# Small-tile matmuls of an attention step in two bursts instead of three

## The chip, the cores and the metric

The kernel runs on one core of a Trainium2 chip. The metric is the device time of one execution in microseconds. Most executions of one kernel agree within about 0.3%; a few here are up to 1% longer, at a granted TensorE clock of 0.989 to 0.996. A profile is one such execution with the hardware profiler on; its span is about 2 us shorter than the time of the run.

## The reference

```python
def _attn_ref(q, k, v):                       # (8, 12, 448, 64) each
    scores = scale * np.matmul(q, k.transpose(0, 1, 3, 2))
    attn = np.maximum(scores, 0.0) ** 2 / S   # squared relu, no softmax
    return np.matmul(attn, v)
...
def _moe_ref(x, w_tok1, w_tok2, w_ch1, w_ch2):  # x: (8, 448, 768), from the heads
    h = np.maximum(x.transpose(0, 2, 1) @ w_tok1, 0.0) @ w_tok2   # over tokens
    u = x + h.transpose(0, 2, 1)
    return u + np.maximum(u @ w_ch1, 0.0) @ w_ch2                 # over channels
```

## The kernel before

The work goes in 24 steps of four heads. In each step run at once: seven score tiles of this step, the values product of the step before (its inputs are squared relus), the transposes of q and k for the next step, and the two token products of the step before. Two channel layers fill TensorE in between: "first-layer" units of 6 matmuls with 448 columns (ScalarE takes the result out of PSUM) and "second-layer" units of 12 with 384 (VectorE takes it). Scores, values and q/k transposes use 64x64 tiles of the array, four at a time, and so does the last part of the first token product in steps 7 and later; all else uses the array whole. TensorE's results land in a memory called PSUM. A channel unit takes one of two banks of it, called "bank" in the code and token banks below; the unit after the next needs the same bank, and can start only when the result has been taken out (evicted).

```python
# PSUM: score tiles 2 x 2 banks, acc0 and acc1 one bank each, two token banks ("bank")
ps_att = ...tile_pool(name="ps_att", bufs=2, space=PSUM)
ps_acc = ...tile_pool(name="ps_acc", bufs=1, space=PSUM)
ps_mm  = ...tile_pool(name="ps_mm", bufs=2, space=PSUM)

def scores(i, c, alone=False):          # 4 matmuls 64*64 into one of two buffers
    ...
    if alone: nc.vector.tensor_scalar(out=at, in0=ps[:, :, :S], scalar1=0.0, ..., op0=ALU.max)
    else:     nc.scalar.activation(at, ps[:, :, :S], AF.Relu)
    squares.append(at)

def square(keep=0):                     # VectorE, in place
    while len(squares) > keep: ...

def fill(share, least=0, upto=0):       # as many channel units as the share asks for
    ...

for i in range(DB + 1, ND + 2):         # steps 4 to 25; "slow" is i <= 6
    scores(i, 0); scores(i, 1)
    values(i - 1, range(QC)); values_out(i - 1)
    scores(i, 2)
    ...                                 # first filler
    square()
    if i - 1 >= XDMA: fill(0.37, least=1)
    scores(i, 3); scores(i, 4)
    transposes(i + 1)                   # into acc0, acc1; both copies on VectorE
    square()
    if slow: token1(i - 1); fill(1 / 3, least=1)
    else:    fill(0.37, least=1, ...); token1_main(i - 1)
    if not slow: token1_rest(i - 1)
    scores(i, 5); scores(i, 6)
    if not slow: square(); fill(0.1, least=1)
    token2(i - 1)                       # its addition is VectorE's
    square()
    fill(1 / 3 if slow else 0.16, least=1)
```

(The step is cut: the conditions at both ends, the loads and the transposes of x are left out.)

Of the kernel before, what the change touches and what calls it, by code (L numbers as in the profile page):

```python
# [16 lines left out]
def kernel(  # L17
# [19 lines left out]
    ND = B * H // 4  # L37
    DB = H // 4
    QC = S // 64
# [83 lines left out]
    qkT, at2, squares, accs = {}, {}, [], {}  # L123
# [60 lines left out]
    def scores(i, c, alone=False):  # L184
        sb = qkT[i]
        ps = ps_att.tile([128, 2, 512], FP32, tag="att", name="sc_ps")
        for r in range(2):
            for g in range(2):
                h = slice(64 * g, 64 * (g + 1))
                nc.tensor.matmul(  # L190
                    ps[64 * r : 64 * (r + 1), g, :S],
                    lhsT=sb[h, r, 1, c * 64 : (c + 1) * 64],
                    rhs=sb[h, r, 0, :],
                    start=True,
                    stop=True,
                    skip_group_check=True,
                )
        at = attn.tile([128, 2, S], BF16, name="at", bufs=12)
        if alone:
            nc.vector.tensor_scalar(  # L200
                out=at, in0=ps[:, :, :S], scalar1=0.0, scalar2=None, op0=ALU.max
            )
        else:
            nc.scalar.activation(at, ps[:, :, :S], AF.Relu)  # L204
        squares.append(at)
        at2[i, c] = at

    def square(keep=0):
        while len(squares) > keep:
            at = squares.pop(0)  # L210
            nc.vector.tensor_tensor(out=at, in0=at, in1=at, op=ALU.mult)  # L211

    def values(i, cs):
        v_raw = raws[i, "v"]
        if i not in accs:
            accs[i] = [ps_acc.tile([128, 512], FP32, tag=f"acc{r}", name="acc_ps") for r in range(2)]
        ps = accs[i]
        for c in cs:
            at = at2.pop((i, c))
            for r in range(2):  # L220
                for g in range(2):
                    h = slice(64 * r, 64 * (r + 1))
                    nc.tensor.matmul(  # L223
                        ps[r][64 * g : 64 * (g + 1), :S],
                        lhsT=v_raw[h, g, c, :],
                        rhs=at[h, g, :],
                        start=(c == 0),
                        stop=(c == QC - 1),
                        skip_group_check=True,
                    )  # L230

    def values_out(i, split=False):
        b, d = divmod(i, DB)
        ps = accs.pop(i)
        for r in range(2):
            if split and r == 1:
                nc.scalar.activation(
                    xT[b % 2][:, 2 * d + r, :S], ps[r][:, :S], AF.Copy, scale=float(alpha2)
                )
                continue  # L240
            nc.vector.tensor_scalar(  # L241
                out=xT[b % 2][:, 2 * d + r, :S],
                in0=ps[r][:, :S],
                scalar1=float(alpha2),
                scalar2=None,
                op0=ALU.mult,
            )
        if i > 2 * DB - 1:
            for r in range(2):
                nc.vector.tensor_scalar(  # L250
                    out=xT[b % 2][:, 2 * d + r, S:],
                    in0=ps[r][:, S - 64 : S],
                    scalar1=float(alpha2),
                    scalar2=None,
                    op0=ALU.mult,
                )
# [3 lines left out]
    XDMA = 8  # L260
# [28 lines left out]
    def token1(i):  # L289
        x_sb = x_tiles.pop(i)  # L290
        ps = ps_mm.tile([128, JC, 256], FP32, tag="bank", name="t1_ps")
        for j in range(JC):
            for c in range(4):
                nc.tensor.matmul(  # L294
                    ps[:, j, :],
                    lhsT=wt1[:, c, j * 128 : (j + 1) * 128],
                    rhs=x_sb[:, :, c, :],
                    start=(c == 0),
                    stop=(c == 3),
                )  # L300
        r1 = mix.tile([128, JC, 256], BF16, name="r1_sb")
        nc.scalar.activation(r1, ps, AF.Relu)
        r1_tiles[i] = r1

    def token1_main(i):
        x_sb = x_tiles[i]
        t1s[i] = ps = [
            ps_acc.tile([128, 512], FP32, tag=f"acc{j}", name="t1_ps2") for j in range(JC)
        ]
        for j in range(JC):  # L310
            for c in range(3):
                nc.tensor.matmul(  # L312
                    ps[j][:, :256],
                    lhsT=wt1[:, c, j * 128 : (j + 1) * 128],
                    rhs=x_sb[:, :, c, :],
                    start=(c == 0),
                    stop=False,
                    skip_group_check=True,
                )

    def token1_rest(i):

        x_sb, ps = x_tiles.pop(i), t1s.pop(i)
        for m in range(2):
            cols = slice(64 * m, 64 * (m + 1))
            for j in range(JC):
                h = slice(64 * j, 64 * (j + 1))
                nc.tensor.matmul(  # L328
                    ps[j][cols, :256],
                    lhsT=wt1_last[h, cols] if j else wt1[h, 3, cols],  # L330
                    rhs=x_sb[h, :, 3, :],
                    start=False,
                    stop=True,
                    skip_group_check=True,
                )
        r1 = mix.tile([128, JC, 256], BF16, name="r1_sb")
        for j in range(JC):
            nc.scalar.activation(r1[:, j, :], ps[j][:, :256], AF.Relu)  # L338
        r1_tiles[i] = r1
# [179 lines left out]
    def fill(share, least=0, upto=0):  # L519
        if not queue:  # L520
            return
        credit[0] += share * rate[0]
        done = 0
        while queue and (credit[0] > 0 or done < least or since[0] < upto):
            cost, unit = queue.pop(0)
            credit[0] -= cost
            since[0] += cost
            unit()
            done += 1


# [70 lines left out]
    i = DB  # L602
# [31 lines left out]
    for i in range(DB + 1, ND + 2):  # L634
        slow = i <= 2 * DB
        back = i - 1 < ND
        if i == 2 * DB + 1:
            rate[0] = (EC * C1 + NT * C2) / DB
        if i < ND:
            scores(i, 0)  # L640
            scores(i, 1)
        if 0 <= i - 1 < ND:
            values(i - 1, range(QC))
            values_out(i - 1)
        if i < ND:
            scores(i, 2)
        if i - 1 < XDMA:
            fill(1 / 3, least=1)
        if 0 <= i - 1 < ND:
            x_back(i - 1)  # L650
        since[0] = 0.0
        if i > 2 * DB + 1:
            if i == 2 * DB + 2:
                hold_back(1, x_tiles[i - 1][:1, 0, 0, :1])
            while u_later and u_later[0] < max(i - 1 - (i == 2 * DB + 2), 0):
                u_back(u_later.pop(0))
        if i + PRE < ND:
            if i - 1 >= XDMA:
                nc.gpsimd.tensor_copy(gate, x_tiles[i - 1][:1, 1, 3, 127:])  # L659
            load_four(i + PRE)  # L660
        if i == 5:
            load_wc2(1, 2)
            load_wt1_last()
        square()
        if i - 1 >= XDMA:
            fill(0.37, least=1)
        if i < ND:
            scores(i, 3)
            scores(i, 4)
        if i + 1 < ND:  # L670
            transposes(i + 1)
        square()
        if slow:
            token1(i - 1)
            fill(1 / 3, least=1)
        else:
            fill(0.37, least=1, upto=4400 if back else 0)
            if back:
                token1_main(i - 1)
        if i < ND:  # L680
            if not slow:
                token1_rest(i - 1)
            scores(i, 5)
            scores(i, 6)
        elif back:
            token1_rest(i - 1)
        if not slow:
            square()
            fill(0.1, least=1)
        if back:  # L690
            token2(i - 1)
            if (i - 1) % DB == DB - 1:
                channel_work((i - 1) // DB)
        if i == 2 * DB + 1:
            hold_back(0, uT_tiles[1][:1, 0, :1])
            for _ in range(DB):
                u_back(u_later.pop(0))
        square()
        fill(1 / 3 if slow else 0.16, least=1)
# [32 lines left out]
```

## Time and profile before

| | before |
|---|---|
| median time | 376.2 us |
| TensorE busy | 365.0 of 374.7 us |
| VectorE, ScalarE busy | 212.1, 211.0 us |
| steps 4 to 6 (41.5 to 69.75 us) | 28.25 us, TensorE busy 28.07 |

Below, "burst" is a run of small-tile matmuls without a whole-array one in it. Its length is the difference of two starts in the timeline: its first score tile's and that of the whole-array matmul behind it. In the kernel before, the first burst of a step takes 2.02 us (202.86 to 204.88 in the lines that the prediction shows) and the second 0.98 (206.94 to 207.92). A length counts the way out of the small tiles, but not the way in, 0.10. One joined burst has one way in less, so it is compared with 2.02 + 0.98 + 0.10 = 3.10 us.

Seven steps have a wait in the first burst. This is the timeline of one (start, length, engine, line, idle before):

```profile
229.89 0.63 DVE L211 TENSOR_TENSOR at<-at 128x896 bf16<-128x896 bf16 x1 [0.19 <-ACT at L204]
230.43 1.15 DVE L363 TENSOR_TENSOR uT_sb<-h_ps,xT 128x448 bf16<-128x448 f32 x2
...
231.32 1.83 PE L223 MATMUL acc_ps<-at,v_raw 64*64 64x448 bf16 x28
```

VectorE squares the score tiles 5 and 6 first, and stands idle before each until ScalarE's relu is done (the square shown is the second). The token addition (L363) follows and ends at 231.58. The values product wants acc0 and acc1, which the addition empties, and takes 1.83 us where it takes 1.49 without that wait. The burst becomes 2.35 us instead of 2.02.

### The profile page before, as it was taken

Reading aid. Unit: us, or ns where it says so; the run is one execution under the profiler, and the core shown is the slowest. Engines: PE = TensorE matmul, PEld = TensorE weight load, DVE = VectorE, ACT = ScalarE, POOL = GpSimd, SP = SyncE. Lnnn points to the kernel's source line nnn. Section 1 sums busy time; section 2 is a strip of 40 time slices with the busy share of each in tenths; the row PEclk is TensorE's granted clock in tenths of the full one; section 3 lists DMA queues with packets and bytes.
Section 4 is the critical chain, followed back from the end, with each engine's and each line's share of the span. In section 5 each row is a group of like instructions: output and inputs, shape, how many; then the busy total and the mean of one; then the engine's idle time right before and its main releaser. Section 6 shows DMA issues by size and latency. Waiting matters only on the chain.

```text
span 374.7 us, 10236 instructions
## 1 busy us (share of the span) xinstructions
PE 365.0 (97%) x4377; PEld 201.2 (54%) x4377; DVE 212.1 (57%) x414; ACT 211.0 (56%) x313; POOL 99.1 (26%) x185
## 2 busy tenths in 40 slices
PE   7889999999999999999999999999999999999996
PEld 3544555455555655565455655555555654555554
DVE  2986688756576666475554684575555755131022
ACT  3987888776345468725775457752775456311400
POOL 8956348304212403430330304412210000000000
PEclk9999999999999999999999999999999999999999
DMA  8999999923998886756765877758560534233024
GB/s 150 118 197 163 179 206 172 180 39 67 128 174 171 159 146 95 115 104 154 97 101 90 117 141 132 108 80 158 107 99 13 93 87 98 58 69 87 0 54 116
DMA packets 69566, 43.32 MB, mean 116 GB/s; under 512 B 43473, under 2 KB 66065, under 8 KB 69521
## 3 DMA queue, kind: packets, MB, share of 16 engines
q0 software_dynamic: 24496, 21.49, 40.8%
q1 hardware_dynamic: 44640, 20.75, 26.6%
q8 instruction: 34, 0.56, 0.6%
q10 hardware_dynamic: 384, 0.43, 0.4%
q14 instruction: 12, 0.09, 0.1%
HBM read 43.42 MB, written 11.01 MB: 145 GB/s over the span
## 4 chain that ended last, share of the span: by engine, by line
PE 89%; DVE 6%; ACT 1%; DMA 1%; issue 1%; POOL 0%; ACTq 0%; POOLq 0%; DVEq 0%
PE m_ps L443 29%; PE m_ps L404 28%; PE acc_ps L223 9%; PE sc_ps L190 9%; PE h_ps L353 4%; PE t_ps L312 3%; DVE at L211 2%; PE qkT_ps L140 2%; PE t_ps L294 1%; DMA q_raw<-in_q_dram 1%; DVE uT_sb L363 1%; PE t_ps L328 1%; ACT at L204 1%; DVE qkT L154 1%; PE x_ps L276 1%
## 5 line engine op out<-in xcount | busy, mean ns | idle before, releaser
L204 ACT ACTIVATE at<-sc_ps 128x896 bf16<-128x896 f32 x167 | 144.8, 924 | 49.7 <-PE sc_ps L190 49.7
L211 DVE TENSOR_TENSOR at<-at 128x896 bf16<-128x896 bf16 x168 | 97.7, 619 | 55.9 <-ACT at L204 55.9
L404 PE MATMUL m_ps<-uT_sb,wc 128*128 128x448 bf16 x564 | 115.5, 353 | 0.2 <-DVE uT_sb L363 0.2
L443 PE MATMUL m_ps<-wc,r_sb 128*128 128x384 bf16 x660 | 113.2, 326 | 0.0
L443 PEld LDWEIGHTS <-r_sb 128*128 128x128 bf16 x660 | 62.7, 98 | 46.7 <-issue 6.1
L411 ACT ACTIVATE r_sb<-m_ps 128x448 bf16<-128x448 f32 x94 | 51.3, 546 | 56.0 <-PE m_ps L404 55.6
L404 PEld LDWEIGHTS <-wc 128*128 128x128 bf16 x564 | 52.3, 98 | 53.4 <-issue 8.3
L450 DVE TENSOR_TENSOR out_sb<-m_ps,u_sb 128x384 f32<-128x384 f32 x55 | 30.5, 554 | 48.1 <-PE m_ps L443 48.1
L190 PE MATMUL sc_ps<-qkT 64*64 64x448 bf16 x672 | 53.2, 358 | 1.1 <-ACT at L204 0.9
L223 PE MATMUL acc_ps<-at,v_raw 64*64 64x448 bf16 x672 | 40.7, 351 | 1.5 <-DVE x_sb L285 0.7
L241 DVE TENSOR_SCALAR xT<-acc_ps 128x448 bf16<-128x448 f32 x45 | 26.1, 620 | 27.6 <-PE acc_ps L223 27.6
L659 POOL COPY gate<-x_sb 1x1 bf16<-1x1 bf16 x12 | 3.1, 254 | 126.9 <-DMA x_sb<-xT 126.9
L83 POOL DMA_DIRECT2D q_raw<-in_q_dram x48 | 28.9, 614 | 19.9 <-DMA wc<-in_moe_w_ch_dram 17.4
L363 DVE TENSOR_TENSOR uT_sb<-h_ps,xT 128x448 bf16<-128x448 f32 x48 | 27.7, 616 | 9.4 <-PE h_ps L353 9.3
L83 POOL DMA_DIRECT2D v_raw<-in_v_dram x48 | 29.6, 643 | 8.1 <-DMA wc<-in_moe_w_ch_dram 4.7
L338 ACT ACTIVATE r_sb<-t_ps 128x256 bf16<-128x256 f32 x36 | 11.8, 381 | 32.7 <-PE t_ps L328 28.5
L223 PEld LDWEIGHTS <-v_raw 64*64 64x64 bf16 x672 | 21.4, 106 | 15.7 <-issue 5.7
L190 PEld LDWEIGHTS <-qkT 64*64 64x64 bf16 x672 | 17.6, 105 | 21.9 <-issue 19.0
L83 POOL DMA_DIRECT2D k_raw<-in_k_dram x46 | 28.2, 634 | 1.7 <-issue 1.7
L154 DVE COPY qkT<-qkT_ps 128x896 bf16<-128x896 bf16 x44 | 25.3, 616 | 5.4 <-PE qkT_ps L140 5.4
L353 PE MATMUL h_ps<-wt,r_sb 128*128 128x448 bf16 x96 | 22.3, 353 | 0.0
L312 PE MATMUL t_ps<-x_sb,wt 128*128 128x256 bf16 x108 | 14.7, 273 | 0.0
(58 smaller groups left out, 150.7 us busy)
## 6 DMA issues: line engine op xcount, KB each, us to landing
out_dram<-out_sb SPq DMA_DIRECT2D x54, 192.0 KB, 2.9
q_raw<-in_q_dram POOLq DMA_DIRECT2D x48, 112.0 KB, 3.9
v_raw<-in_v_dram POOLq DMA_DIRECT2D x48, 112.0 KB, 4.8
k_raw<-in_k_dram POOLq DMA_DIRECT2D x46, 112.0 KB, 4.4
wc<-in_moe_w_ch_dram POOLq DMA_DIRECT2D x4, 1152.0 KB, 12.2
u_sb<-uT_sb SPq DMA_TRANSPOSE x48, 2.6
x_sb<-xT SPq DMA_TRANSPOSE x16, 3.2
k_first<-in_k_dram SPq DMA_DIRECT2D x1, 224.0 KB, 3.5
```

The costliest lines, as they stand in the source:

```text
L83: eng.dma_start(out=dst[64 * r : 64 * (r + 1)].rearrange("p g c d -> p g (c d)"), in_=src[b, h0 : h0 + 2].rearrange("g (p c) d -> p g (c d ...
L154: (nc.scalar.copy if split and r == 0 else nc.vector.tensor_copy)(sb[:, r].rearrange("n w t -> n (w t)"), parts[r][:, : 2 * S])
L190: nc.tensor.matmul(ps[64 * r : 64 * (r + 1), g, :S], lhsT=sb[h, r, 1, c * 64 : (c + 1) * 64], rhs=sb[h, r, 0, :], start=True, stop=True, s ...
L204: nc.scalar.activation(at, ps[:, :, :S], AF.Relu)
L211: nc.vector.tensor_tensor(out=at, in0=at, in1=at, op=ALU.mult)
L223: nc.tensor.matmul(ps[r][64 * g : 64 * (g + 1), :S], lhsT=v_raw[h, g, c, :], rhs=at[h, g, :], start=(c == 0), stop=(c == QC - 1), skip_gro ...
L353: nc.tensor.matmul(parts[r][:, :S], lhsT=r1[:, j, r * 128 : (r + 1) * 128], rhs=wt2[:, j, :], start=(j == 0), stop=(j == JC - 1),)
L363: nc.vector.tensor_tensor(out=uT_tiles[b // 2][:, 2 * d + r, off : off + S].rearrange("n (c p) -> n c p", c=QC), in0=parts[r][:, :S].rearr ...
L404: nc.tensor.matmul(ps[:, :S], lhsT=wc1[:, g, e * 128 : (e + 1) * 128], rhs=uT[:, g, off : off + S], start=(g == 0), stop=(g == CC - 1),)
L411: nc.scalar.activation(r2[:, e, off : off + S], ps[:, :S], AF.Relu)
L443: nc.tensor.matmul(ps[:, :HN], lhsT=r2[:, e, t * 128 : (t + 1) * 128], rhs=wc2[:, e, cols], start=(e == 0), stop=(e == EC - 1),)
L450: nc.vector.tensor_tensor(out=o[:, cols].rearrange("n (g d) -> n g d", d=128), in0=ps[:, :HN].rearrange("n (g d) -> n g d", d=128), in1=u_ ...
```

## The change

The intent is to enter and leave the small tiles twice a step, not three times. The transposes go into the token banks, so that they need not wait for the values product to leave acc0 and acc1. The values product is cut in two, to give relus time between score tiles. Score tiles 1 and 3 go to VectorE, and one transpose copy and one values copy to ScalarE. Each channel unit now also queues one square.

```diff
@@ fill
             unit()
+            square(keep=max(len(squares) - 1, 0))
@@ the step
             scores(i, 0)
-            scores(i, 1)
-        if 0 <= i - 1 < ND:
-            values(i - 1, range(QC))
-            values_out(i - 1)
+            scores(i, 1, alone=True)
+        if i + 1 < ND and not slow:
+            transposes(i + 1, "bank", split=True)
+        if back:
+            values(i - 1, (0, 1, 2))
         if i < ND:
             scores(i, 2)
+        if back:
+            values(i - 1, (3, 4, 5, 6))
+            values_out(i - 1, split=True)
+        if i < ND:
+            scores(i, 3, alone=True)
+            scores(i, 4)
 ...
-        square()
-        if i - 1 >= XDMA:
-            fill(0.37, least=1)
-        if i < ND:
-            scores(i, 3)
-            scores(i, 4)
-        if i + 1 < ND:
+        if slow:
+            fill(1 / 3, least=1)
+            token1(i - 1)
             transposes(i + 1)
-        square()
-        if slow:
-            token1(i - 1)
-            fill(1 / 3, least=1)
         else:
-            fill(0.37, least=1, upto=4400 if back else 0)
+            far = back and i - 1 >= XDMA
+            fill(0.74 if far else 0.4, least=1, upto=4400 if far else 0)
             if back:
                 token1_main(i - 1)
+                token1_rest(i - 1)
         if i < ND:
-            if not slow:
-                token1_rest(i - 1)
             scores(i, 5)
             scores(i, 6)
-        elif back:
-            token1_rest(i - 1)
-        if not slow:
-            square()
-            fill(0.1, least=1)
+        fill(0.1, least=1)
         if back:
             token2(i - 1)
```

## The prediction

> **What bounds the kernel now.** I read the page first, then the busy time by stretches, then the timeline of one step, then the waits.
>
> ```profile
> span 374.7 us, 10236 instructions
> PE 365.0 (97%) x4377; PEld 201.2 (54%) x4377; DVE 212.1 (57%) x414; ACT 211.0 (56%) x313; POOL 99.1 (26%) x185
> ...
> PE 89%; DVE 6%; ACT 1%; DMA 1%; issue 1%; POOL 0%; ACTq 0%; POOLq 0%; DVEq 0%
> ```
>
> TensorE is busy for 97% of the span and holds 89% of the chain that ended last. By stretches (columns: window, length, then busy time of PE, PEld, DVE, ACT, POOL; granted clock, DMA share, GB/s):
>
> ```profile
> 39.00:72.00 33.00, 32.82 (x508) 17.86 (x507) 25.91 (x47) 28.15 (x40) 15.29 (x26) 1.00 1.16 190
> ...
> 90.00:310.00 220.00, 219.96 (x2696) 121.98 (x2688) 134.94 (x270) 124.07 (x184) 51.15 (x96) 1.00 0.69 115
> ```
>
> In 90 to 310 us TensorE never rests; VectorE is 61% and ScalarE 56% busy. In 39 to 72 us (the three "slow" steps) TensorE is just as full, but ScalarE is at 85% and VectorE at 79%: little room. So TensorE's stream is the time, and a change gains only by shortening it and loses by any wait put into it. A step handles four heads: seven score tiles (L190, relu on L204, square on L211), the values product of the step before (L223), transposes for the next (L140), two token products (L312 with L328, and L353), and between them channel units of 6 (L404) or 12 (L443) matmuls as filler. One step's timeline (start, length, engine, line):
>
> ```profile
> 202.86 0.57 PE L190 MATMUL sc_ps<-qkT 64*64 64x448 bf16 x8
> 203.26 1.49 PE L223 MATMUL acc_ps<-at,v_raw 64*64 64x448 bf16 x28
> 204.59 0.36 PE L190 MATMUL sc_ps<-qkT 64*64 64x448 bf16 x4
> 204.88 2.12 PE L443 MATMUL m_ps<-wc,r_sb 128*128 128x384 bf16 x12
> 206.94 0.57 PE L190 MATMUL sc_ps<-qkT 64*64 64x448 bf16 x8
> 207.34 0.39 PE L140 MATMUL qkT_ps<-ident,q_raw 64*64 64x64 bf16 x28
> 207.56 0.43 PE L140 MATMUL qkT_ps<-ident,k_raw 64*64 64x64 bf16 x28
> 207.92 4.07 PE L443 MATMUL m_ps<-wc,r_sb 128*128 128x384 bf16 x24
> 211.83 0.82 PE L312 MATMUL t_ps<-x_sb,wt 128*128 128x256 bf16 x6
> ```
>
> Ends are modelled, so I use differences of starts. 24 channel matmuls take 211.83 - 207.92 = 3.91 us, 0.163 each; 12 of them (1.956) followed by score tiles take 206.94 - 204.88 = 2.06: 0.10 us goes into the change from full to 64x64 tiles. Back again: two score tiles take 207.34 - 206.94 = 0.40, or 0.20 each, but the single one before a channel block 204.88 - 204.59 = 0.29: another 0.09. A round trip costs 0.19 us, and a step makes three.
>
> **What the Trainium skill says.** (1) "TensorEngine Tiling (Array Packing)", Key Properties: changing the tiling mode drains TensorE. The trace agrees, at 0.19 us a round trip. (2) "Perfetto Trace Analysis", Tensor Engine Instruction: TensorE can pull weight loads ahead, while VectorE and ScalarE are strict first-in, first-out. The trace fits: no VectorE instruction overtakes its program order. (3) "TensorEngine Tiling (Array Packing)", PSUM Bottleneck: tiling speeds up TensorE but not the emptying of PSUM, which may then be the limit. Before, no burst has more than three score tiles, and TensorE waits for ScalarE there only 0.9 us in total.
>
> **The change part by part.** *Removed:* bursts of small tiles go from three a step to two, in steps 4 to 23: 20 x 0.19 = -3.8 us. Matmul and channel-unit counts stay. *Work moved:* per ordinary step two score tiles go to VectorE, and one transpose copy and one values copy go to ScalarE. Durations before:
>
> ```profile
> L204 ACT ACTIVATE at<-sc_ps 128x896 bf16<-128x896 f32 x167 | 144.8, 924 | 49.7 <-PE sc_ps L190 49.7
> ...
> L411 ACT ACTIVATE r_sb<-m_ps 128x448 bf16<-128x448 f32 x94 | 51.3, 546 | 56.0 <-PE m_ps L404 55.6
> ...
> L285 ACT COPY x_sb<-x_ps 128x1024 bf16<-128x1024 bf16 x1 | 1.1, 1085 | 0.0
> L200 DVE TENSOR_SCALAR at<-sc_ps 128x896 bf16<-128x896 f32 x1 | 1.1, 1084 | 0.0
> ```
>
> A score tile costs 1.08 on VectorE against 0.92 on ScalarE; a 128x896 transpose copy 0.62 on VectorE and, estimated from the 1.085 of 128x1024, 0.96 on ScalarE; a values copy 0.62 or 0.575. Net VectorE +0.93 a step, ScalarE -0.3. Both have room on average; order decides.
>
> *New wait 1, the banks.* The transposes now stand right behind score tiles 0 and 1, in both token banks, so they need the last two channel units of the step before emptied. Set zero at score tile 0; unstalled, the transposes start at 0.40. If the last unit is a first-layer one (L404), its last matmul ends at +0.07, ScalarE takes it from about 0.11 to 0.65, and the transposes start at 0.70: wait 0.30. If it is a second-layer unit (L443), VectorE takes it, behind what the new order has queued. A unit now pops only one square, and all squares left over stand between the token addition and the last unit's eviction. Walk with three left, with the durations that the timeline before shows where they run back to back (1.15 for two additions, 1.68 for three squares, 0.55 for an eviction or a square): the next-to-last unit's eviction starts at -2.60 (unit 1.96, second token product 0.76, last unit 2.04 before zero), 0.55; square 0.55; two token additions 1.15; three squares 1.68; last eviction 0.55: ends at +1.88, transposes at 1.94, wait 1.54. With two left 0.97; with one left 0.32 to 0.41. From the changed order: one step has three left before 3 bursts (after steps 9, 10, 16), two before 2 (after 13, 19), one before 3 (after 8, 15, 21); 7 follow a first-layer unit (after 7, 11, 12, 14, 17, 18, 20). Sum: 3 x 1.54 + 2 x 0.97 + 1.05 + 7 x 0.30 = 9.7 us.
>
> *New wait 2, the fifth score tile.* There are two score buffers, so tile 4 waits for tile 2's relu, which stands behind tile 0's relu and the transpose copy on ScalarE. With transposes at t: the copy runs from t + 0.72 to t + 1.68, the relu to t + 2.55, tile 4 at 2.60 instead of t + 2.24: 0.36 in each of those 15 bursts, 5.4 us. Step 23 has no transposes, but the same backlog holds tile 3 back: 1.0.
>
> *Removed waits.* Before, after first-layer steps, values and the third score tile wait 0.16 + 0.18 for a late token addition; the chain shows 7 such steps (values 1.66 instead of 1.32). Now the addition is earlier: -2.4.
>
> *Slow steps.* Four fills instead of three a step take four units each in steps 4 and 5; the eight prepared ones are then gone, and step 6 has none until its end (in the built order too). Step 4: tile 2 waits for tile 0's relu behind an L411, tile 4 for tile 2: 0.75. Step 5: the same, and tile 3's buffer waits for VectorE, which first works off four squares: 1.16. Step 6: nothing hides the chain values copy, score tile on VectorE, x copy (0.69), first token product, transpose copies (1.15), token addition: I walk it to 9.65 us where its matmuls need 6.75; 2.9, less the 0.34 that it had. All seven squares follow: in step 7 values wait until 3.4 us and tile 3 until 4.5, 2.06 in all. Sum +6.5.
>
> *Total:* 9.7 + 5.4 + 1.0 + 6.5 - 3.8 - 2.4 = +16.4, so 392.5. As walks by hand count some overlap twice, I take 391.
>
> **The rivals.** (A) Only the saving arrives: VectorE and ScalarE are under 62% busy in the long stretch, and the design spreads squares behind units. That gives 372. Against it: averages do not see the queue at one moment, and the built order puts the additions and squares ahead of the last eviction. (B) The waits exist in the ordinary steps, but slow steps absorb theirs, or the ScalarE copy is cheaper than 0.96: about 384. (C) A wait for the transposed x (3.4 to 5.2 us from issue to landing) replaces the saving: the values copy comes later, and in steps of first-layer units alone I find 0.7 us of margin where there was 1.6; if it goes, another 2 to 4 us: 395. (D) VectorE becomes the bound: its 61% plus 0.93 us a step of some 14 stays under 70%, so not on average.
>
> **Range and chances.** Floor: the bank wait of 0.30 and tile 4's wait nearly cancel the saving and the removed waits, and step 6 loses some us whatever else holds: 380. Ceiling with (C): 398. Slower by over 2% begins at 383.6; (B) or smaller waits would stay under it. Faster 0.03, within 2% 0.19, slower 0.78.
>
> **What would show it.** In the changed profile: one round trip fewer a step leaves TensorE's work about as it was, so the span grows by its idle time; the idle time stands at the transposes, put down to the last unit's eviction (VectorE 1 to 1.5 us after L443, ScalarE 0.3 after L411); idle before score tile 4 put down to ScalarE; a hole of about 3 us in step 6 and 2 us in step 7, near 63 to 75 us. I am wrong if transposes start 0.4 us after score tile 0, if VectorE has done its squares before the last unit ends, or if step 6 keeps TensorE full.

## The result, and the profile after

The changed kernel takes 390.56 us (median; 390.36 to 391.37), the kernel before 376.17. The ratio is 1.039, 95% interval 1.037 to 1.041: slower. Here and below, a ratio is the mean time of one kernel's fast runs over that of the other's of the same rounds, so not quite the ratio of the medians that are quoted.

The page of the changed kernel (span 388.6 us), its busy line and the chain of work that ended last:

```profile
PE 367.1 (94%) x4377; PEld 203.8 (52%) x4377; DVE 233.1 (60%) x417; ACT 202.2 (52%) x310; POOL 100.8 (26%) x185
...
PE 70%; DVE 19%; ACT 7%; issue 3%; ACTq 0%; DVEq 0%
```

TensorE has the same 4377 matmuls and nearly the same busy time. But its part of the chain fell from 89% to 70%, and VectorE's rose from 6% to 19%, though VectorE is busy only 60% of the span. An engine that is idle for 40% of the span is now on the path, which suggests that what matters is when it does a thing, not how much it does; the runs below test that. By stretches (the slow steps 4 to 6, step 7, and the long stretch; columns as in the prediction):

```profile
41.00:73.50 32.50, 29.00 (x451) 16.00 (x450) 25.20 (x40) 20.88 (x30) 14.02 (x24) 1.00 1.08 175
73.50:88.30 14.80, 13.54 (x171) 7.03 (x170) 11.41 (x22) 9.36 (x15) 2.34 (x8) 1.00 0.34 46
90.00:310.00 220.00, 211.98 (x2574) 119.31 (x2564) 141.10 (x255) 117.73 (x183) 52.06 (x96) 1.00 0.63 110
```

TensorE now has holes in all three: 3.5 us in the slow steps, which also take 32.5 us instead of 28.25; 1.3 in step 7; 8.0 in the long stretch, where it had none. Who made it wait (total, times, longest; short waits of under 0.15 us are not in this view):

```profile
PE sc_ps L190 <- ACT at L204: 4.6, 21, 0.5
PE qkT_ps L140 <- DVE out_sb L450: 4.4, 5, 1.1
PE t_ps L294 <- DVE x_sb L285: 1.5, 2, 1.0
PE sc_ps L190 <- DVE at L200: 1.2, 3, 0.6
```

The second line is the wait of the transposes for a bank. One of the worst bursts in order of time:

```profile
119.31 0.56 DVE L450 TENSOR_TENSOR out_sb<-m_ps,u_sb 128x384 f32<-128x384 f32 x1 [2.29 <-issue]
...
119.78 0.61 DVE L211 TENSOR_TENSOR at<-at 128x896 bf16<-128x896 bf16 x1
...
120.31 1.15 DVE L363 TENSOR_TENSOR uT_sb<-h_ps,xT 128x448 bf16<-128x448 f32 x2
121.38 1.68 DVE L211 TENSOR_TENSOR at<-at 128x896 bf16<-128x896 bf16 x3
...
121.85 0.57 PE L190 MATMUL sc_ps<-qkT 64*64 64x448 bf16 x8
...
122.25 0.20 PE L140 MATMUL qkT_ps<-ident,q_raw 64*64 64x64 bf16 x2
...
122.98 0.55 DVE L450 TENSOR_TENSOR out_sb<-m_ps,u_sb 128x384 f32<-128x384 f32 x1
...
123.58 0.41 PE L140 MATMUL qkT_ps<-ident,q_raw 64*64 64x64 bf16 x26 [1.14 <-DVE out_sb L450]
...
126.40 0.82 PE L443 MATMUL m_ps<-wc,r_sb 128*128 128x384 bf16 x4
```

Two transposes start at 122.25, because their bank is empty; the other 54 wait until 123.58. The last channel unit's results were complete near 121.9, but VectorE, idle for 2.29 us earlier, first did the eviction of the unit before, a square, two additions and three squares, and came to the last eviction (L450) at 122.98. The view counts 1.14 us of idle time, as the end of the two matmuls is modelled; from start to start it is 1.33. The burst takes 126.40 - 121.85 = 4.55 us instead of 3.10.

Burst lengths, from starts, account for the loss from step 4 on:

| part | before | after | difference |
|---|---|---|---|
| steps 4 to 6 | 28.24 | 32.50 | +4.3 |
| burst of step 7 | 3.10 | 4.97 | +1.9 |
| 15 bursts of steps 8 to 22 | 15 x 3.10, and 7 x 0.33 | 56.7 | +7.8 |
| burst of step 23, without transposes | 2.63 | 3.18 | +0.6 |
| channel unit behind the x transposes, steps 7 and 8 | 0 | 2 x 0.25 | +0.5 |
| values product of step 24, which also waited before | 1.98 | 1.73 | -0.3 |

The sum is 14.8. The profiled run came to step 4 0.5 us earlier than that of before, so 14.3 are to be compared with 388.6 - 374.7 = 13.9.

### The profile page after: what moved, and what is told of

Its sections match the earlier page's. It is cut to its first block, busy times and chain, and to the rows that moved or that the text cites. A ratio compares the mean times of both kernels' runs of the same rounds, so it can differ in the third digit from the quotient of the medians.

```text
span 388.6 us, 10179 instructions
## 1 busy us (share of the span) xinstructions
PE 367.1 (94%) x4377; PEld 203.8 (52%) x4377; DVE 233.1 (60%) x417; ACT 202.2 (52%) x310; POOL 100.8 (26%) x185
## 4 chain that ended last, share of the span: by engine, by line
PE 70%; DVE 19%; ACT 7%; issue 3%; ACTq 0%; DVEq 0%
PE m_ps L404 27%; PE m_ps L443 25%; DVE at L211 7%; ACT at L204 5%; PE sc_ps L190 4%; DVE at L200 4%; DVE uT_sb L363 4%; PE t_ps L312 3%; PE h_ps L353 3%; DVE out_sb L450 2%; DVE qkT L154 2%; PE qkT_ps L140 2%; PE t_ps L294 1%; ACT r_sb L411 1%; PE t_ps L328 1%
## 5 line engine op out<-in xcount | busy, mean ns | idle before, releaser
L204 ACT ACTIVATE at<-sc_ps 128x896 bf16<-128x896 f32 x127 | 113.2, 926 | 33.0 <-PE sc_ps L190 31.8
L450 DVE TENSOR_TENSOR out_sb<-m_ps,u_sb 128x384 f32<-128x384 f32 x55 | 30.6, 556 | 76.4 <-PE m_ps L443 71.3
L190 PE MATMUL sc_ps<-qkT 64*64 64x448 bf16 x672 | 55.4, 357 | 6.3 <-ACT at L204 4.6
L223 PE MATMUL acc_ps<-at,v_raw 64*64 64x448 bf16 x672 | 43.0, 351 | 1.7 <-DVE x_sb L285 0.7
L200 DVE TENSOR_SCALAR at<-sc_ps 128x896 bf16<-128x896 f32 x41 | 44.4, 1082 | 0.3 <-PE sc_ps L190 0.2
L667 POOL COPY gate<-x_sb 1x1 bf16<-1x1 bf16 x12 | 4.6, 385 | 132.5 <-DMA x_sb<-xT 132.5
L190 PEld LDWEIGHTS <-qkT 64*64 64x64 bf16 x672 | 21.2, 105 | 28.2 <-issue 24.1
L241 DVE TENSOR_SCALAR xT<-acc_ps 128x448 bf16<-128x448 f32 x24 | 14.9, 622 | 10.4 <-PE acc_ps L223 10.4
L154 DVE COPY qkT<-qkT_ps 128x896 bf16<-128x896 bf16 x28 | 16.7, 614 | 5.1 <-PE qkT_ps L140 5.1
```

Of the source, the lines that this page charges most:

```text
L190: nc.tensor.matmul(ps[64 * r : 64 * (r + 1), g, :S], lhsT=sb[h, r, 1, c * 64 : (c + 1) * 64], rhs=sb[h, r, 0, :], start=True, stop=True, s ...
L223: nc.tensor.matmul(ps[r][64 * g : 64 * (g + 1), :S], lhsT=v_raw[h, g, c, :], rhs=at[h, g, :], start=(c == 0), stop=(c == QC - 1), skip_gro ...
L450: nc.vector.tensor_tensor(out=o[:, cols].rearrange("n (g d) -> n g d", d=128), in0=ps[:, :HN].rearrange("n (g d) -> n g d", d=128), in1=u_ ...
```

## The experiments

My theory: the order on VectorE and ScalarE, and the PSUM buffers that depend on it, cost the time. Rivals: the extra VectorE work itself; the slow steps alone or the ordinary steps alone; the burst form as such, however it is ordered. All runs but one gave a correct result. The kernel before ran beside each at 376.35 to 376.58 us.

### Slow steps as before

Steps 4 to 6 get their three bursts and three fills back, and units queue no squares there.

```diff
+        pops[0] = not slow                     # fill squares only in ordinary steps
-            scores(i, 1, alone=True)
+            scores(i, 1, alone=not slow)
 ...
+            if slow: values(i - 1, range(QC)); values_out(i - 1)
 ...
         if slow:
-            fill(1 / 3, least=1)
-            token1(i - 1)
-            transposes(i + 1)
+            square(); scores(i, 3); scores(i, 4)
+            transposes(i + 1); square()
+            token1(i - 1); fill(1 / 3, least=1)
```

> The changed kernel with steps 4 to 6 put back as they stood before (three bursts, three fills, squares at once); steps 7 on stay changed. Theory (order and emptied filler queue cost the time there): the trace has these steps at 32.5 us against 28.2 before, and step 7's burst at 5.0 us against about 3.5 in its like; so 4.3 + 1.5 = 5.8 us come back, 384.8 us. Rival (the loss lies in the ordinary steps alone): 390.6 us, unchanged.

Measured: 385.11 us, ratio to before 1.022. 5.4 us came back, against 5.8 expected. The rival falls: more than a third of the loss of 14.4 us was made in three steps that have no filler to spare, and in step 7 behind them, whose burst takes 3.47 us here instead of 4.97. A fourth fill in each step had used the eight prepared units up in steps 4 and 5 and left step 6 bare until its end.

### Squares earlier

```diff
             fill(0.74 if far else 0.4, least=1, upto=4400 if far else 0)
+            square()
             if back:
                 token1_main(i - 1)
```

> The changed kernel, but in ordinary steps all squares in hand are worked off before the first token product, so that one is left behind the token addition instead of up to three. Theory (VectorE's order holds back the last eviction and so the transposes): the waits of 1.3 us in three bursts and 0.73 in two fall to 0.31, 3.8 us, and about 0.5 in step 23; 386.3 us. Rival (VectorE has too much work, whatever the order): the same work, so 390.6 us.

Measured: 386.78 us, ratio 1.027; 3.8 us came back. The same burst as above, in this kernel's timeline:

```profile
122.04 0.62 DVE L211 TENSOR_TENSOR at<-at 128x896 bf16<-128x896 bf16 x1
...
122.51 0.57 PE L190 MATMUL sc_ps<-qkT 64*64 64x448 bf16 x8
122.68 0.56 DVE L450 TENSOR_TENSOR out_sb<-m_ps,u_sb 128x384 f32<-128x384 f32 x1
...
123.29 0.41 PE L140 MATMUL qkT_ps<-ident,q_raw 64*64 64x64 bf16 x26 [0.18 <-DVE out_sb L450]
...
126.10 1.15 PE L443 MATMUL m_ps<-wc,r_sb 128*128 128x384 bf16 x6
```

One square stands before the eviction instead of three, the transposes wait 0.37 us instead of 1.33, and the burst takes 3.59. VectorE does exactly the same work as in the changed kernel. So its order, not its load, made this part.

### Both transpose copies on VectorE

```diff
-            transposes(i + 1, "bank", split=True)
+            transposes(i + 1, "bank")
```

> The changed kernel, but both transpose copies of ordinary steps go to VectorE. My recorded step (the fifth score tile waits because the relu of the third stands behind the transpose copy on ScalarE): the relu starts 0.13 us sooner in 15 bursts, about 2 us, 388.6 us. Rival 1 (the round trip of two score buffers alone sets it, about 1.4 us from tile 2 to tile 4): 390.6 us. Rival 2 (VectorE is the bound): 0.62 us more a step, 395 us or more.

Measured: 389.92 us, ratio 1.035; 0.6 us less than the changed kernel, near rival 1. A burst behind a first-layer unit, first in the changed kernel, then in this one:

```profile
152.74 0.57 PE L190 MATMUL sc_ps<-qkT 64*64 64x448 bf16 x8
...
155.40 0.38 PE L190 MATMUL sc_ps<-qkT 64*64 64x448 bf16 x4
155.94 0.38 PE L190 MATMUL sc_ps<-qkT 64*64 64x448 bf16 x4 [0.17 <-ACT at L204]
156.26 0.93 PE L404 MATMUL m_ps<-uT_sb,wc 128*128 128x448 bf16 x4
```

```profile
153.57 0.57 PE L190 MATMUL sc_ps<-qkT 64*64 64x448 bf16 x8
...
156.23 0.82 PE L190 MATMUL sc_ps<-qkT 64*64 64x448 bf16 x8
156.99 1.31 PE L404 MATMUL m_ps<-uT_sb,wc 128*128 128x448 bf16 x6
```

3.52 against 3.42 us: the copy on ScalarE was only 0.1 us of a wait that I had put down to it wholly. Tile 4 still starts 0.25 us late, 1.39 us behind tile 2 (1.49 in the changed kernel). That I put down to the trip from score tile 2 through its relu to tile 4.

### One burst more

The kernel before, with a channel unit between score tile 4 and the transposes.

```diff
             scores(i, 4)
+        if not slow and i + 1 < ND:
+            fill(0.1, least=1)
         if i + 1 < ND:
             transposes(i + 1)
```

> The kernel before with one burst more a step: a channel unit is put between score tile 4 and the transposes in steps 7 to 22, with no other order changed but the units' places. Theory (a change of tile size and back costs 0.19 us of TensorE): 16 x 0.19 = 3.0 us, 379.2 us. Rival (the drain is hidden, and bursts are free): 376.2 us.

Measured: 381.72 us, ratio 1.013: 5.2 us more, not 3.0. The timeline of one such step:

```profile
108.02 0.57 PE L190 MATMUL sc_ps<-qkT 64*64 64x448 bf16 x8
108.53 2.12 PE L443 MATMUL m_ps<-wc,r_sb 128*128 128x384 bf16 x12
110.58 0.41 PE L140 MATMUL qkT_ps<-ident,q_raw 64*64 64x64 bf16 x28
...
111.16 1.15 PE L443 MATMUL m_ps<-wc,r_sb 128*128 128x384 bf16 x6
```

Score pair 0.51, unit 2.05, transposes 0.58, together 3.14; without the cut they are 0.98 and 12 x 0.163 = 1.96, so the round trip costs 0.20 us, as predicted, or 3.2 us in 16 steps. Of the remaining 2 us, 1.6 are the test's own fault: the extra fill uses the units up sooner, and two holes of about 1.0 and 0.6 us open in step 24, where no unit is left to fill the waits for the transposed x and for a relu. So the saving aimed at is real.

### Only the engines changed

The kernel before in its own order, with the four pieces of work on the engines where the change puts them.

```diff
-            scores(i, 1)
+            scores(i, 1, alone=not slow)
-            values_out(i - 1)
+            values_out(i - 1, split=not slow)
-            scores(i, 3)
+            scores(i, 3, alone=not slow)
-            transposes(i + 1)
+            transposes(i + 1, split=not slow)
```

> The kernel before in its order, with only the engines changed in ordinary steps: score tiles 1 and 3 on VectorE, one transpose copy and one values copy on ScalarE. Theory (engine load is not the bound): 376.2 us within 0.8. Rival (VectorE's 0.93 us more a step is what costs): up to 15 us more, 390 us.

Measured: 376.36 us, ratio 0.9995 (0.995 to 1.004). VectorE's busy time in the long stretch rose from 134.94 to 150.67 us, more than in the changed kernel, at no cost that shows. So the load alone, in the old order, is not what costs.

### Transposes later in the burst

The changed kernel; values 0 to 5 stand before score tile 2, then value 6 and the transposes, then score tiles 3 and 4.

```diff
-        if i + 1 < ND and not slow:
-            transposes(i + 1, "bank", split=True)
-            values(i - 1, (0, 1, 2))
+            values(i - 1, (0, 1, 2) if slow else range(6))
 ...
-            values(i - 1, (3, 4, 5, 6))
+            values(i - 1, (3, 4, 5, 6) if slow else (6,))
+            if i + 1 < ND and not slow:
+                transposes(i + 1, "bank", split=True)
             values_out(i - 1, split=True)
```

> The changed kernel with the transposes moved back inside the burst, behind all values and ahead of score tile 3; squares and slow steps as changed. Theory: the bank waits go (6.3 us by the trace), the fifth tile's wait falls from about 0.44 to 0.2 us (3.6), some 1.5 comes back as a wait of the first channel unit for the transpose copies: 382.5 us. Rival (the waits come from evicting engines that are full, and only move): 389 us or more.

Measured: 384.72 us, ratio 1.021. 5.8 us came back, of the 8.1 that the expected 382.5 stands for (its parts, 6.3 + 3.6 - 1.5, make 8.4). The bank wait is gone from the list of TensorE's waits, and the bursts of steps 8 to 22 take 3.31 to 3.48 us; but they do not reach 3.1. In most of them tile 4 starts 0.54 us behind tile 3, as it did in the changed kernel: that wait did not shrink as I had expected.

### Two bursts, well ordered

Slow steps as before, squares earlier, and transposes late, in one kernel.

> Two bursts in ordinary steps, well ordered: slow steps as before, squares worked off before the first token product, six values, score tile 2, one value, the transposes, then score tiles 3 and 4, with the transpose copies ahead of the values copies. Theory (two score buffers and two evicting engines set the burst: tile 4 still waits some 0.2 us and the first channel unit some 0.1 us, which eats the 0.19 us saved): 376 us, no better than before. Rival (only bad order cost time, the two bursts themselves pay 3.0 us, and the old waits of 2.3 us are gone too): 371 us.

Measured: 378.50 us, ratio 1.006 (1.002 to 1.010). Neither value was met: the kernel is no faster than before, as my theory had it, but it is 2.5 us above my number. The timeline:

```profile
133.59 0.57 PE L190 MATMUL sc_ps<-qkT 64*64 64x448 bf16 x8
...
135.97 0.38 PE L190 MATMUL sc_ps<-qkT 64*64 64x448 bf16 x4
136.51 0.38 PE L190 MATMUL sc_ps<-qkT 64*64 64x448 bf16 x4 [0.16 <-ACT at L204]
136.93 1.29 PE L404 MATMUL m_ps<-uT_sb,wc 128*128 128x448 bf16 x6
```

Tile 4 starts 0.54 us behind tile 3, where 0.19 is the pace, so 0.35 are lost, and the burst is 3.34 us.

### Half a relu

A wrong result: the kernel above, with ScalarE's relu of score tile 2 taking one of its two halves, so that the buffer is free sooner.

```diff
+        if half:
+            nc.scalar.activation(at[:, 0], ps[:, 0, :S], AF.Relu)
+            nc.gpsimd.memset(at[:, 1], 0.0)
```

> A wrong result on purpose: the well ordered two-burst kernel, but ScalarE's relu takes only half of score tile 2 in ordinary steps (GpSimd zeroes the other half, away from PSUM), so that its buffer is free after about 0.55 us in place of 0.94. Theory (the time from tile 2's matmuls through its relu to tile 4, over two score buffers, is what the burst still waits for, 0.35 us in 16 bursts by the trace): that wait nearly goes, -5 us, 373.5 us. Rival (ScalarE and VectorE are full there, and the wait moves to the channel unit behind the burst): 377.5 us or more.

Measured: 377.30 us, 1.2 us less than the kernel above. The theory's 373.5 fails; the rival's 377.5 or more was missed by only 0.2. Its waits:

```profile
PE m_ps L407 <- DVE qkT L154: 3.5, 9, 0.4
PE m_ps L446 <- DVE qkT L154: 2.7, 7, 0.4
```

(L407 and L446 are the two channel layers, whose lines are shifted here.) The wait for the relu went, and 16 waits of 0.4 us took its place: the channel unit behind the burst wants a token bank, from which the transposes had not been copied out yet. The 16 bursts with transposes take 3.31 to 3.38 us, most of them 3.33 as in the kernel above; only step 23's, which has no transposes, fell, from 3.23 to 2.86. The second limit shows already in the lines of the kernel above: the channel unit starts 0.42 us behind tile 4 (136.51 to 136.93), where 0.29 is usual. Two limits lie side by side, and taking one away shows the other.

### Transposes in the middle

So the transposes have to stand late enough for empty banks and early enough to be copied before the burst ends. Against "Two bursts, well ordered":

```diff
-                values(i - 1, range(6))
+                values(i - 1, (0, 1, 2))
+        if i + 1 < ND and not slow:
+            transposes(i + 1, "bank")          # both copies on VectorE
 ...
-            values(i - 1, (6,))
-            transposes(i + 1, "bank", split=True)
+            values(i - 1, (3, 4, 5, 6))
```

> The well ordered two-burst kernel with the transposes between value tile 2 and score tile 2, and both transpose copies on VectorE: the banks are empty by then (0.75 us), and the copies end before the channel units want the banks. Theory (only the two-buffer round trip of about 1.35 us from score tile 2 to 4 is left; burst 3.13 us in place of 3.33): 378.5 - 16 x 0.20 = 375.3 us, no faster than the kernel before beyond noise and slower than that kernel with its squares moved (373.3). Rival (no floor is left and the burst runs at its 2.92 us): 372 us.

Measured: 375.33 us, ratio 0.997 (0.995 to 0.999). A burst:

```profile
120.10 0.57 PE L190 MATMUL sc_ps<-qkT 64*64 64x448 bf16 x8
...
121.07 0.39 PE L140 MATMUL qkT_ps<-ident,q_raw 64*64 64x64 bf16 x28
121.29 0.41 PE L140 MATMUL qkT_ps<-ident,k_raw 64*64 64x64 bf16 x28
121.51 0.38 PE L190 MATMUL sc_ps<-qkT 64*64 64x448 bf16 x4
...
122.46 0.83 PE L190 MATMUL sc_ps<-qkT 64*64 64x448 bf16 x8
123.22 0.99 PE L443 MATMUL m_ps<-wc,r_sb 128*128 128x384 bf16 x5
```

3.12 us here, up to 3.25 elsewhere. That is about the 3.10 of the two separate bursts without their waits. The last score pair takes 0.76 us instead of 0.51. Tile 2 starts 1.41 us behind tile 0, as the relu of that ends (ScalarE, 120.54 to 121.46), and tile 4 as long behind tile 2, so five tiles through two buffers take about 2.8 us, and the way out 0.3 more. The whole saving of two bursts is about as large as this wait. What the kernel gains, 1.0 us, is less than the 2.3 of the waits of before that went. (The profiled run was the slowest of seven, 378.10 us at a clock of 0.994; it came to step 4 2.4 us later than the kernel before, so its excess lies ahead of the bursts.) Not tested: a shorter relu in this order, which would show whether the trip is the only limit left, and the place of the transposes apart from the engine of their copies, which were changed together.

### The kernel before, squares 5 and 6 behind the addition

```diff
         if not slow:
-            square()
             fill(0.1, least=1)
```

> The kernel before with one line moved: in ordinary steps squares 5 and 6 are queued on VectorE behind the token addition instead of ahead of it. Theory (order on VectorE alone made values and the third score tile wait 0.33 us in 7 steps, which the change had removed): -2.3 us, 373.9 us. Rival (those waits are made up for elsewhere): 376.2 us.

Measured: 373.31 us, ratio 0.991 (0.988 to 0.994): the fastest of all. The step shown for the kernel before, now:

```profile
227.50 1.16 DVE L363 TENSOR_TENSOR uT_sb<-h_ps,xT 128x448 bf16<-128x448 f32 x2 [4.01 <-PE h_ps L353]
...
228.57 1.15 DVE L211 TENSOR_TENSOR at<-at 128x896 bf16<-128x896 bf16 x2
...
229.31 1.49 PE L223 MATMUL acc_ps<-at,v_raw 64*64 64x448 bf16 x28
```

The addition no longer stands behind squares that wait for ScalarE, and in steps 8 to 23 every first burst takes 2.01 to 2.02 us. One line of the three-burst kernel was worth more than the two bursts: both kernels are free of those waits, and the one with three bursts is about 2 us faster.

## Why the prediction was right

391.0 was predicted and 390.6 measured. By its own steps:

- *What bounds the kernel:* right. TensorE's stream is the time, and the change lost by waits put into it.
- *Removed round trips, 3.8 us:* the 0.19 is right for the cut it was read from (0.20 in the run with one burst more), but joining these bursts saves more. 56 transposes take 0.58 us when a whole-array matmul follows (207.34 to 207.92), and 0.44 when small tiles do (121.07 to 121.51 in the run with the transposes in the middle). So a joined burst without waits is 0.40 + 0.44 + 1.33 + 0.19 + 0.19 + 0.29 = 2.84 us, 0.26 less than 3.10, and not the 2.92 that an expectation used.
- *Engines, "order decides":* right. Moving the work alone cost nothing (376.36), and working squares off earlier took 3.8 us off with the same work.
- *The banks, 9.7 us:* the mechanism is right, the term somewhat too large. From the starts in the trace the waits are 1.27 to 1.33 us in three bursts (predicted 1.54), 0.74 in two (0.97) and 0.30 to 0.32 in ten, 8.4 us in all. The long ones are shorter because I added full durations where VectorE's instructions overlap a little (the first square starts 0.47 us behind the eviction, which lasts 0.56). The 6.3 us that an expectation names is the same reading against the 0.58 of the transposes, so it is net of 0.14 us a burst that belongs to the saving above.
- *The fifth score tile, 5.4 us:* the size is right, the reason only in part. I said that the relu stands behind the transpose copy. That is 0.1 us of 0.35; the trip through two score buffers, which no run tests by itself, is my reading of the rest.
- *Step 23, 1.0 us:* 0.8 by the same reading (3.18 us against 2.41 without a wait).
- *Slow steps, 6.5 us:* 4.3 and 1.9 in the trace are net of four saved round trips (0.8), which makes 6.9; putting the steps back gave 5.4 of it. Step 7's burst was predicted at 2.92 + 2.06 = 4.98 and took 4.97. Not foreseen: the unit behind the x transposes waits 0.25 us for a bank, in steps 4, 5, 7 and 8.
- *Removed waits, 2.4 us:* right; the run that removes these alone gained 3.3 by the medians, 2.3 of it in these bursts, and 0.5 in an eighth wait of the same kind, in step 24 (its values product: 1.98 us before, 1.45 then).
- *The rivals:* (A), the saving alone, fell with the result. (B), that slow steps absorb their part, fell with the run that puts them back. (C), a wait for the transposed x, is not among the changed kernel's waits. (D), VectorE as the bound, fell with the run that moves work alone.
- *The total:* that 391.0 lies within half a us of the result is partly luck. The parts summed to 392.5, and 1.5 were taken off by a guess that walks count some overlap twice. They did, in the banks (1.3 too much); but the saving was also about 1 us too small and the slow steps some tenths too cheap, and these errors nearly cancel.

What stays open: 0.4 us of the sum that I could not place, and some 0.5 us more than the waits explain in the fastest kernel's gain.

## What to carry to other kernels

Before you join bursts on the engine that is the bound, count what the joined burst asks of its buffers: tiles per burst, the trip from matmul through eviction, and who else wants the same banks. On an engine that empties buffers in program order, put the work that frees a buffer ahead of work that nobody waits for; where it stands counts more than how busy the engine is. And when a fix takes a wait away without gaining, look for the second limit beside it, as the half relu showed.

## What the Trainium skill lacked or had wrong

- "TensorEngine Tiling (Array Packing)", Key Properties: it says that a change of tiling mode drains TensorE, but no cost. Here it is 0.10 us into 64x64 tiles and 0.09 to 0.11 out of them behind score tiles, 0.14 behind transposes (0.58 less 0.44).
- "Perfetto Trace Analysis", Optimization Strategy: equal gaps that repeat can mean too little PSUM. The 0.35 us before score tile 4 fits that, though no run had more score buffers. It does not say that the same gap comes from an eviction in the wrong place of a queue: 1.33 us before the transposes fell to 0.37 with no buffer added.
- No page has what a transpose of 64x64 costs in a packed stream: 56 of them took 0.44 us with small tiles behind them, and 0.58 with a whole-array matmul behind.
